# Attention and two mixture layers: scores of two tiles at once, steps in a new order, four first loads on ScalarE's queue

## The chip, the cores and the metric

The kernel runs on one core of a Trainium2 chip. A core has five engines with queues of their own: TensorE (PE: matmuls; PEld is its loading of weights), VectorE (DVE), ScalarE (ACT), GpSimd (POOL) and SyncE (SP, which here only issues DMAs). Each works through its instructions in order and waits for the others at semaphores; 16 DMA engines move data between memory (HBM) and the core's buffers. The metric is the time of one execution on the device in microseconds; lower is better.

## What is computed

Three layers follow each other. The first is attention within chunks of 64 positions, 8 batches of 8 heads; the second a soft mixture of experts over all 4608 tokens, whose two softmaxes run over tokens and over slots; the third a wide layer with a product of softmax and input and a normalization.

```python
scores = scale * np.matmul(q_c, k_c.transpose(0, 1, 2, 4, 3))
scores = scores - np.max(scores, axis=-1, keepdims=True)
attn = np.exp(scores)
attn = attn / (np.sum(attn, axis=-1, keepdims=True) + 1e-09)
out = np.matmul(attn, v_c)
...
logits = x @ phi
d = softmax of logits over tokens;  slot_input = d.T @ x
h = np.maximum(slot_input[e] @ w1[e], 0.0);  slot_out[e] = h @ w2[e]
x = softmax of logits over slots @ slot_out
...
h = x @ w_in;  solu = h * softmax(h)
ln = (solu - mean) / np.sqrt(var + 1e-06) * g_ln
out = ln @ w_out
```

## The kernel before

Tokens are cut into 36 tiles of 128 (`NT`), a tile holding two chunks for all 8 heads. A loop of 34 steps (L517) carries the attention in a software pipeline: in step i the scores of tile i are made, the probabilities of tile i-1 turned, the output x of tile i-2 made, and x of tile i-3 turned and multiplied with `phi`. Nothing reorders the work: each engine executes what the program text issues, in that order. Within a step the text's order is given by one of four lines of the table `STEP` (L29), taken in turn, so a pattern repeats every four steps. The names in a line are small functions, listed in `step_ops` (L471):

- `S` (TensorE) scores of a tile into the PSUM tile `s_ps`; `mx`, `sub` (VectorE) row maxima and their subtraction; `exp` (ScalarE); `PT` (TensorE) turns the probabilities and `PTe` (ScalarE) copies them out of PSUM; `x` (TensorE) multiplies with v; `rz` (ScalarE) copies the row sums, `rc` (VectorE) takes the reciprocal and `xm` (VectorE) multiplies; `xT`, `xTe` turn x and copy it.
- Every fourth step has work on a block of four tiles: `LT`, `lte`, `L`, `lall`, `tm`, `mT`, `mn`, `d`, `de`, `z`, `sl`, `acc`, which keep the running softmax over tokens and its weighted sum of x.
- `t`, `sq` (ScalarE), `u`, `a` (VectorE), `m`, `add`, `mul` (GpSimd) convert the third layer's weights, one chunk a step, from the tile `raw`.
- `qk`, `v`, `raw` and `W` issue loads on SyncE: q and k of tile i+4 (two DMAs of 256 KB), v of two tiles, two chunks of raw weights, and as many 512 KB loads of expert weights as the table `PACE` gives for the step.

The scores alternate between two banks of one PSUM tile `sx` (L249). `qk` may be issued when the scores that read the same one of four buffers are done. `FIRST` (L44) lists the loads ahead of the loop, all on SyncE. Behind the loop a list `ORDER` names the rest by hand: tiles 32 to 35, the experts (64 loads of weights, used by `h_ps` groups at L936, L973 and L987 up to 183 us), and from about 200 us the third layer, whose tiles are handled by a second loop at L1421.

Of the kernel before, what the change touches and what calls it, by code (L numbers as in the profile page):

```python
# [9 lines left out]
F32 = mybir.dt.float32  # L10
# [3 lines left out]
U32 = mybir.dt.uint32  # L14
# [3 lines left out]
PSUM = bass.MemoryType.PSUM  # L18
# [8 lines left out]


STEP = """  # L29
S a m t x xT u mT qk rz PT mx v xTe sub PTe W rc add mul raw exp xm mn d sq de  # L30
S a x u raw v m qk rz sl mx t W rc z xT sub xTe PT PTe add xm acc mul sq exp
m t S u a x qk rz xT mx W sub xTe PT rc acc v PTe add LT xm mul sq raw exp lte
t m a S x u raw L tm v mx xT add qk PT lall rz mul xTe sub rc PTe W sq xm exp
"""
PACE = [
    0, 0, 0, 0, 0, 0, 0, 1, 2, 2, 3, 4, 4, 5, 6, 6, 7, 8, 8, 9, 10, 10, 11, 12, 13, 13, 14, 15,
# [4 lines left out]
""".split()  # L41
AHEAD = 8
GATE = dict()
FIRST = "cs qk0 qk1 qk2 v0 raw0 qk3 g phi v2 raw2 raw4"  # L44
ORDER = """
cq1 cq2 cq3 cq4 cq5 cq6 cq7 S34 S35 loadw xT31 mx34 mx35 PT33 x32 xtev31 rz32 ptev33 sub34 LT31 lte7 ev32 own_c exp34
x33 own_q PT34 ptev34 xT32 L7 rz33 sub351 sub350 x34 exp350 PT350 exp351 ev33 xtev32 ptev0 xT33 PT351 lall7 LT32 rz34
# [20 lines left out]
def soft_moe_kernel(ctx: ExitStack, tc, qkT, v1, w12, w64, phi, g_ln, cst, out):  # L68
    nc = tc.nc
    ts = lambda i, n: slice(i * n, (i + 1) * n)  # L70

    def pool(name, bufs, stack=ctx, **kw):
        kw.setdefault("reuse_waits", "tile")
        return stack.enter_context(tc.tile_pool(name=name, bufs=bufs, **kw))
# [4 lines left out]
    cs = const.tile([128, 257], F32, name="cs")  # L79
# [5 lines left out]
    phi_sb = const.tile([128, 4, 32], F32, name="phi_sb")  # L85
    g_sb = const.tile([128, 8], F32, name="g_sb")
# [10 lines left out]
    lall = mp.tile([128, NT, 32], F32, name="lall")  # L97
    acc = mp.tile([128, 512], F32, name="acc")
# [6 lines left out]
    def mark(key, r):  # L105
        LAST[key] = r.ins.name

    def gated(what, r):
        key = GATE.get(what)
        if key in LAST:  # L110
            info = mybir.DependencyInfo(mybir.DependencyClass.Sync, mybir.DependencyReason.DATA)
            tc.add_manual_dep(r.ins, LAST[key], info, reason="even pace of loads")
# [45 lines left out]
    ps1 = pool("ps1", 1, p1, space=PSUM)  # L158
# [4 lines left out]
    qk = [cvp.tile([128, 3, 512], F32, name=f"qk{i}") for i in range(4)]  # L163
# [3 lines left out]
    vall = cvb.tile([128, 6, 520], F32, name="vall")  # L167
# [2 lines left out]
    zacc = kvp.tile([128, 1], F32, name="zacc")  # L170
    csum = kvp.tile([128, 512], F32, name="csum")

    def load_qk(t):
        if t < NT:
            for a in range(2):
                nc.sync.dma_start(out=qk[t % 4][a:128:2, a:a + 2, :], in_=qkT[t, a])


    def load_v(t):
        if t < NT and t % 2 == 0:  # L180
            gated("v", nc.sync.dma_start(out=vall[:, t % 6:t % 6 + 2, :].rearrange("p a d -> p (a d)"), in_=v1[t // 2]))

    raw_t = {}

    def load_raw(c):
        if c < NRAW and c % 2 == 0:
            raw = cvp.tile([128, 2, 256, 2], U32, tag="raw", name="raw", bufs=3)
            raw_t[c], raw_t[c + 1] = raw[:, 0], raw[:, 1]
            gated("raw", nc.sync.dma_start(out=raw.rearrange("p k n t -> p (k n t)"), in_=w64[c // 2].bitcast(U32)))

# [19 lines left out]
    def cv_u(c):  # L212
        mark("u", nc.vector.tensor_scalar(
            out=cv(c, "cu"), in0=cv_hi(c), scalar1=3, scalar2=0x3FFFFFF8, op0=ALU.logical_shift_left, op1=ALU.bitwise_and
        ))
# [11 lines left out]
    def cv_s(c):  # L227
        u = cvt["cu", c]
        nc.gpsimd.tensor_tensor(out=u, in0=u, in1=cvt["cr", c], op=ALU.add)  # L229
# [5 lines left out]
    def cv_c(c):  # L235
        nc.gpsimd.tensor_tensor(out=csum, in0=csum if c > 1 else wo[:, 0, :], in1=wo[:, c, :], op=ALU.add)

    first_loads = dict(
        qk0=lambda: load_qk(0), qk1=lambda: load_qk(1), qk2=lambda: load_qk(2), qk3=lambda: load_qk(3), v0=lambda: load_v(0), v2=lambda: load_v(2),
        **{f"raw{i}": lambda i=i: load_raw(i) for i in range(6)},  # L240
        cs=lambda: nc.sync.dma_start(out=cs, in_=cst), phi=lambda: nc.sync.dma_start(out=phi_sb, in_=phi),
        g=lambda: nc.sync.dma_start(out=g_sb, in_=g_ln),
    )
    for o in FIRST.split():
        first_loads[o]()

    p_t, pt_t, xps_t, x_t, lt_t, sps_t, mx_t = {}, {}, {}, {}, {}, {}, {}

    sx = ps1.tile([128, 2, 512], F32, name="s_ps")  # L249

    def pe_S(i):
        s = sx[:, i % 2, :]
        b = qk[i % 4]
        for g in range(4):
            for c in range(2):
                nc.tensor.matmul(  # L256
                    s[ts(c, 64), ts(g, 128)], b[:, 1, ts(2 * g + c, 64)], b[:, 0:3:2, ts(2 * g + c, 64)],
                    start=True, stop=True, tile_position=(0, 64 * c),
                )
        sps_t[i] = s.rearrange("p (h k) -> p h k", k=64)  # L260
# [28 lines left out]
    def x_view(x):  # L289
        return x[:, :, 0:260].rearrange("p a (g d) -> p a g d", d=65)  # L290

    def heads(x):
        return x.rearrange("p (g a d) -> p a g d", a=2, d=64)
# [8 lines left out]
    def x_sums(xp):  # L302
        rz = sm.tile([128, 2, 4, 1], F32, tag="rz", name="rz", bufs=4)
        nc.scalar.activation(out=rz, in_=xp[:, :, :, 64:65], func=AF.Copy, bias=1e-9)
        return rz
# [165 lines left out]
    def step_ops(i):  # L471
        s0, s1, s2, s3, s4 = (blk(n, i) for n in (6, 7, 8, 9, 10))
        if i == NT - 3:
            s4 = s3
        c = cstep.get(i, NRAW)
        st = {}

        def rz():
            st["xp"] = x_view(xps_t[i - 2])
            st["rz"] = x_sums(st["xp"])  # L480

        def rc():
            mark("rc", nc.vector.reciprocal(out=st["rz"], in_=st["rz"]))

        def xm():
            x_t[i - 2] = x = XB[(i - 2) % 7]
            mark("xm", nc.vector.tensor_tensor(
                out=heads(x), in0=st["xp"][:, :, :, 0:64],
                in1=st["rz"].to_broadcast([128, 2, 4, 64]), op=ALU.mult,
            ))  # L490

        def W():
            load_w(pace[i + 1] - pace[i])

        cvc, x2, x3 = c < NRAW, i >= 2, i >= 3
        return dict(
            u=(cvc, lambda: cv_u(c)), m=(cvc, lambda: cv_m(c)), a=(cvc, lambda: cv_a(c)), add=(cvc, lambda: cv_s(c)),
            mul=(cvc, lambda: cv_w(c)), raw=(cvc, lambda: load_raw(c + 5)),
            sq=(True, lambda: cv_sq(cstep.get(i + 1, NRAW))), t=(True, lambda: cv_t(cstep.get(i + 1, NRAW))),
            S=(True, lambda: pe_S(i)), qk=(True, lambda: load_qk(i + 4)),  # L500
            mx=(True, lambda: soft_max(i)), sub=(True, lambda: soft_sub(i)), exp=(True, lambda: exp_S(i)),
            PT=(i >= 1, lambda: PTm(i - 1)), PTe=(i >= 1, lambda: PTe(i - 1)),
            x=(x2, lambda: pe_x(i - 2)), v=(i >= 1, lambda: load_v(i + 3)),
            rz=(x2, rz), rc=(x2, rc), xm=(x2, xm),
            xT=(x3, lambda: xTm(i - 3)), xTe=(x3, lambda: xTe(i - 3)), LT=(x3, lambda: pe_LT(i - 3)),
            lte=(s0 is not None, lambda: blk_a(s0)),
            L=(s1 is not None, lambda: pe_L(s1)), lall=(s1 is not None, lambda: blk_l(s1)),
            tm=(s1 is not None, lambda: run_max(s1)),
            mT=(s2 is not None, lambda: mTm(s2)), mn=(s2 is not None, lambda: mnv(s2)),
            d=(s2 is not None, lambda: dv(s2)),  # L510
            de=(s2 is not None, lambda: de(s2)),
            z=(s3 is not None, lambda: zm(s3)), sl=(s3 is not None, lambda: slm(s3)),
            acc=(s4 is not None, lambda: blk_e2(s4)), W=(True, W),
        )
# [9 lines left out]
    n, last = NT - 1, NB - 1  # L524
# [53 lines left out]


    def x34():  # L580
        xps_t[n - 1] = x = sx
        pt = pt_t.pop(n - 1)
        for g in range(4):
            x_mm(n - 1, x, pt[:, g, :], g)
# [185 lines left out]
    def pt_pair():  # L770
# [79 lines left out]
    def sim(hf):  # L850
# [10 lines left out]
        out=siT,  # L861
# [415 lines left out]
    for n_ in range(2):  # L1277
# [18 lines left out]
        out=F["e1"], in_=F["h1"], func=AF.Exp, bias=F["nm1"][0], scale=1.0, accum_out=F["zz1"][:, 0:1]))  # L1296
# [201 lines left out]
```

## Time and profile before

| | us |
|---|---|
| median of 3 runs | 403.44 (402.84 to 403.8) |
| the profiled execution | 402.77 |
| its span, first to last instruction | 401.0 |

The page says of the span: TensorE is busy for 382.4 us, VectorE 311.0, ScalarE 224.3, GpSimd 200.2; 70.60 MB are read from HBM. In the slices a digit is the busy share in tenths of one fortieth of the span, 10 us. Matmul records overlap in a pipeline, so that the start of one group to the start of the next is the better measure of what a group costs TensorE than its own duration; a group of scores has 16 records.

### The profile page before, as it was taken

The page shows a single profiled execution, that of the slowest core. Times are in us where ns is not written, and L with a number is a line of the kernel's source. Part 1 is how long each engine was busy: PE and PEld are TensorE (multiplying, and loading weights), DVE is VectorE, ACT ScalarE, POOL GpSimd, SP SyncE. Part 2 cuts the span into 40 slices and gives each one's busy share as a digit, 9 for nine tenths or more (in the row PEclk, how much of TensorE's full clock was granted, in tenths as well). Part 3 has the DMA queues.
Part 4 walks back from the last instruction along what each step waited for, and adds up shares of the span by engine and source line. Part 5 has one row for each costly group of instructions (what it writes and reads, how often), then busy time and mean ns, then how long its engine had stood idle before and what let it go on. Part 6 is the DMA issues. An engine that isn't in the chain of part 4 may idle for free. (4 is left out here: it accounts for less than half of the span.)

```text
span 401.0 us, 10317 instructions
## 1 busy us (share of the span) xinstructions
PE 382.4 (95%) x3947; PEld 220.4 (55%) x3947; DVE 311.0 (78%) x777; ACT 224.3 (56%) x470; POOL 200.2 (50%) x201
## 2 busy tenths in 40 slices
PE   3799899999999999999999999999999999999997
PEld 2577777777787642354544444444444444444445
DVE  3788788989886449574989799999888888888840
ACT  1577877877785512332577765556554555455521
POOL 2577767777778246330123255555455544454430
PEclk9999999999999999999999999999999999999999
DMA  7999999999999999991156757777665666557671
GB/s 231 403 409 408 389 397 397 409 407 407 410 397 408 401 396 406 409 391 26 30 103 146 140 134 159 159 158 148 144 140 135 144 151 133 132 137 158 132 159 52
DMA packets 101153, 99.20 MB, mean 247 GB/s; under 512 B 78064, under 2 KB 78704, under 8 KB 101104
## 3 DMA queue, kind: packets, MB, share of 16 engines
q1 hardware_dynamic: 101104, 98.54, 77.1%
q8 instruction: 31, 0.51, 0.5%
q14 instruction: 18, 0.15, 0.1%
HBM read 70.60 MB, written 9.44 MB: 200 GB/s over the span
## 5 line engine op out<-in xcount | busy, mean ns | idle before, releaser
L1194 POOL TENSOR_SCALAR uh<-u,sc 128x1024 f16<-128x1024 f32 (+1 forms) x35 | 65.1, 1860 | 51.1 <-issue 38.3
L1393 PEld LDWEIGHTS <-uhT 128*128 128x128 f16 x560 | 52.1, 98 | 68.3 <-issue 8.8
L1393 PE MATMUL o_ps<-xb,uhT 128*128 128x512 f16 x280 | 66.7, 380 | 0.7 <-DMA uhT<-uh 0.7
L1393 PE MATMUL o_ps<-xb,ulT 128*128 128x512 f16 x280 | 66.3, 379 | 0.0
L1393 PE MATMUL o_ps<-wo,uhT 128*128 128x512 f16 x280 | 66.1, 379 | 0.0
L1322 ACT ACTIVATE e<-h_ps,nm 128x1024 f32<-128x1024 f32 x34 | 37.8, 1113 | 43.7 <-DVE nm L1316 43.7
L1210 ACT ACTIVATE e<-u,nmean 128x1024 f32<-128x1024 f32 x35 | 40.1, 1147 | 28.7 <-DVE nmean L1209 28.7
L256 PE MATMUL s_ps<-qk 128*64 128x128 f32 x576 | 41.1, 287 | 9.3 <-DMA qk<-in_qkT 6.5
L1360 POOL TENSOR_TENSOR a<-a,mhalf 128x1 f32<-128x1 f32 x36 | 21.8, 606 | 56.2 <-DVE a L1377 42.5
L1316 DVE TENSOR_REDUCE nm<-h_ps 128x1 f32<-128x1024 f32 x34 | 41.5, 1220 | 9.3 <-PE h_ps L1311 9.3
L1185 DVE SCALAR_TENSOR_TENSOR u<-h_ps,e 128x1024 f32<-128x1024 f32 x35 | 42.8, 1223 | 6.1 <-ACT e L1322 6.1
L1393 PEld LDWEIGHTS <-ulT 128*128 128x128 f16 x280 | 27.3, 98 | 33.1 <-issue 0.3
L1370 DVE SCALAR_TENSOR_TENSOR ul<-u,sc,uh 128x1024 f16<-128x1024 f32 x35 | 45.3, 1295 | 0.0
L256 PEld LDWEIGHTS s_ps<-qk 128*64 128x64 f32 x576 | 32.5, 141 | 16.2 <-issue 10.3
L398 ACT ACTIVATE xt_b<-xt_ps 128x512 f32<-128x512 f32 (+1 forms) x37 | 21.6, 586 | 17.8 <-PE xt_ps L416 16.9
L265 DVE TENSOR_REDUCE mx<-s_ps 128x8 f32<-128x512 f32 x36 | 24.6, 684 | 8.5 <-PE s_ps L256 8.0
L1411 ACT ACTIVATE ob<-o_ps,a 128x512 f32<-128x512 f32 x35 | 23.8, 679 | 9.3 <-PE o_ps L1393 8.0
L219 POOL TENSOR_SCALAR conv<-conv 128x256 f32<-128x256 f32 x16 | 17.6, 1099 | 21.8 <-ACT conv L206 21.8
L1311 PE MATMUL h_ps<-s,c4T 128*128 128x512 f32 x68 | 27.4, 485 | 0.0
L277 ACT ACTIVATE p<-p 128x512 f32<-128x512 f32 x35 | 21.7, 621 | 6.6 <-DVE p L271 6.6
L271 DVE TENSOR_TENSOR p<-s_ps,mx 128x512 f32<-128x512 f32 x35 | 24.1, 690 | 0.9
L229 POOL TENSOR_TENSOR conv<-conv 128x256 int32<-128x256 int32 x32 | 23.3, 729 | 2.6
(232 smaller groups left out, 633.5 us busy)
## 6 DMA issues: line engine op xcount, KB each, us to landing
w<-in_w SPq DMA_DIRECT2D x45, 512.0 KB, 8.0
qk<-in_qkT SPq DMA_DIRECT2D x72, 256.0 KB, 6.8
vall<-in_v SPq DMA_DIRECT2D x18, 520.0 KB, 6.7
out<-ob SPq DMA_DIRECT2D x35, 256.0 KB, 2.1
raw<-in_w SPq DMA_DIRECT2D x16, 512.0 KB, 6.4
qk<-in_w SPq DMA_DIRECT2D x4, 512.0 KB, 9.0
w_raw<-in_w SPq DMA_DIRECT2D x3, 512.0 KB, 9.0
vall<-in_w SPq DMA_DIRECT2D x3, 512.0 KB, 8.9
```

Of the source, the lines that this page charges most:

```text
L256: nc.tensor.matmul(s[ts(c, 64), ts(g, 128)], b[:, 1, ts(2 * g + c, 64)], b[:, 0:3:2, ts(2 * g + c, 64)], start=True, stop=True, tile_posit ...
L265: mark("mx", nc.vector.tensor_reduce(out=mx, in_=s, axis=AX.X, op=ALU.max))
L271: mark("sub", nc.vector.tensor_tensor(out=p, in0=s, in1=mx.unsqueeze(2).to_broadcast([128, 8, 64]), op=ALU.subtract,))
L1185: nc.vector.scalar_tensor_tensor(out=u, in0=d["h"], scalar=1.0, in1=e, op0=ALU.mult, op1=ALU.mult, accum_out=zz[:, 1:2])
L1194: nc.gpsimd.tensor_scalar(out=uh[:, 0:n], in0=u[:, 0:n], scalar1=d["sc"][:, 1:2], scalar2=1.0, op0=ALU.mult, op1=ALU.mult)
L1210: nc.scalar.activation(out=d["e"], in_=d["u"], func=AF.Square, bias=nmean, scale=1.0, accum_out=d["zz"][:, 2:3])
L1311: nc.tensor.matmul(h[:, ts(n, 512)], c4T[:, i, :], s4[n], start=True, stop=True)
L1316: nc.vector.tensor_reduce(out=nm, in_=st[i]["h"], axis=AX.X, op=ALU.max, negate=True)
L1322: nc.scalar.activation(out=d["e"], in_=d["h"], func=AF.Exp, bias=d["nm"], scale=1.0, accum_out=d["zz"][:, 0:1])
L1370: nc.vector.scalar_tensor_tensor(out=ul, in0=d["u"], scalar=d["sc"][:, 1:2], in1=d["uh"], op0=ALU.mult, op1=ALU.subtract)
L1393: nc.tensor.matmul(d["o"], lt(n % 8), w(n % 8), start=(n == 0), stop=(n == 23))
L1411: nc.scalar.activation(out=ob, in_=d["o"], func=AF.Copy, scale=d["a"][:, 7:8])
```

## The change

`S` is now called in even steps only and makes the scores of tiles i and i+1, one behind the other; each has a PSUM tile of its own (`s0` and `s1`, in a pool `ps_s`). The pool is closed ahead of the x of tile 34 and one with the old tile `sx` opened in its place. All four lines of `STEP` have a new order. Of the first loads, q and k of tiles 2 and 3 go into ScalarE's queue (marked `*`), and three loads leave the list: the second v and raw are issued right behind the q and k of step 0, the third raw behind those of step 1 (`THEN`).

```diff
 STEP = """
-S a m t x xT u mT qk rz PT mx v xTe sub PTe W rc add mul raw exp xm mn d sq de
-S a x u raw v m qk rz sl mx t W rc z xT sub xTe PT PTe add xm acc mul sq exp
-m t S u a x qk rz xT mx W sub xTe PT rc acc v PTe add LT xm mul sq raw exp lte
-t m a S x u raw L tm v mx xT add qk PT lall rz mul xTe sub rc PTe W sq xm exp
+S x t v m a rz xT u qk xTe PT mT PTe mx W sub add rc exp mul xm mn sq d raw de
+S mx xT qk x PT a u sub z m W raw add PTe rz sl exp t rc mul xm v acc xTe sq
+S m mx t x u W a acc xT rz PT xTe raw add LT mul sub rc PTe v sq exp lte qk xm
+x u S qk a m v t add rz mx sub xT L raw PT tm PTe rc xTe mul xm lall sq exp W
 """
...
-FIRST = "cs qk0 qk1 qk2 v0 raw0 qk3 g phi v2 raw2 raw4"
+FIRST = "cs qk0 qk1 qk2* v0 raw0 qk3* g phi"
+THEN = {0: 'v2 raw2', 1: 'raw4'}
...
-                nc.sync.dma_start(out=qk[t % 4][a:128:2, a:a + 2, :], in_=qkT[t, a])
+                queue[0].dma_start(out=qk[t % 4][a:128:2, a:a + 2, :], in_=qkT[t, a])
...
     for o in FIRST.split():
-        first_loads[o]()
+        queue[0] = nc.scalar if o[-1] == "*" else nc.sync
+        first_loads[o.rstrip("*")]()
+    queue[0] = nc.sync
...
-    sx = ps1.tile([128, 2, 512], F32, name="s_ps")
+    pss = ctx.enter_context(ExitStack())
+    ps_s = pool("ps_s", 1, pss, space=PSUM)
+    s_banks = [ps_s.tile([128, 512], F32, name="s_ps", tag=f"s{a}") for a in range(2)]
+    sx = None
...
-        s = sx[:, i % 2, :]
+        s = s_banks[i % 2]
...
+        def q():
+            load_qk(i + 4)
+            for o in THEN.get(i, "").split():
+                first_loads[o]()
...
-            S=(True, lambda: pe_S(i)), qk=(True, lambda: load_qk(i + 4)),
+            S=(i % 2 == 0, lambda: (pe_S(i), pe_S(i + 1))), qk=(True, q),
...
     def x34():
+        nonlocal sx
+        pss.close()
+        sx = pool("ps_sx", 1, pss, space=PSUM).tile([128, 2, 512], F32, name="s_ps")
```

In the rows of order that follow, a name with a number is one buffer (`qk0_111` is the buffer of every fourth tile's q and k), and xN is how many instructions of the kind stand in a row; the line numbers of the changed kernel are some 8 higher.

TensorE in the loop, the first two steps of a pattern of four, before: one group of scores at the front of each step.

```order
L256 MATMUL s_ps_148<-qk0_111 64x128 x8
L282 MATMUL x_ps_1121<-vall_123,pt_1103 64x65 x16
L416 MATMUL xt_ps_1138<-cs_60,xb6_86 128x128 x4
L423 MATMUL mT_ps_1144<-cs_60,ltb_149 128x128
L407 MATMUL pt_ps_1150<-cs_60,p_1100 128x128 x4
L256 MATMUL s_ps_148<-qk1_112 64x128 x8
L282 MATMUL x_ps_1188<-vall_123,pt_1160 64x65 x16
L467 MATMUL sl_ps_1214<-xb1_81,d_1170 32x512
```

The same two steps on TensorE after:

```order
L264 MATMUL s_ps_146<-qk0_111 64x128 x8
L264 MATMUL s_ps_147<-qk1_112 64x128 x8
L290 MATMUL x_ps_1130<-vall_123,pt_1103 64x65 x16
L424 MATMUL xt_ps_1152<-cs_60,xb6_86 128x128 x4
L415 MATMUL pt_ps_1161<-cs_60,p_1086 128x128 x4
L431 MATMUL mT_ps_1166<-cs_60,ltb_148 128x128
L424 MATMUL xt_ps_1193<-cs_60,xb0_80 128x128 x4
L290 MATMUL x_ps_1200<-vall_123,pt_1168 64x65 x16
L415 MATMUL pt_ps_1217<-cs_60,p_1174 128x128 x4
L469 MATMUL lt_ps_1028<-cs_60,d_1183 128x1
L475 MATMUL sl_ps_1235<-xb1_81,d_1183 32x512
```

The second scores have moved to the front of the first step, and the second step begins with the turning of `xb0_80`, made from the x of the step before, which used to stand behind x, sl and z.

SyncE at the start, before, from the constants to the q and k of tile 4 (which go to the buffer `qk0_111` again):

```order
L241 DMA cs_60<-in_cst 128x257
L176 DMA qk0_111<-in_qkT 64x1024 x2
L176 DMA qk1_112<-in_qkT 64x1024 x2
L176 DMA qk2_113<-in_qkT 64x1024 x2
L181 DMA vall_123<-in_v1 128x1040
L189 DMA raw_137<-in_w64 128x1024
L176 DMA qk3_114<-in_qkT 64x1024 x2
L242 DMA g_sb_62<-in_g_ln 128x8
L241 DMA phi_sb_61<-in_phi 128x128
L181 DMA vall_123<-in_v1 128x1040
L189 DMA raw_144<-in_w64 128x1024
L189 DMA raw_146<-in_w64 128x1024
```

SyncE at the start after, up to the q and k of tile 5 (buffer `qk1_112`) and the third raw:

```order
L244 DMA cs_60<-in_cst 128x257
L179 DMA qk0_111<-in_qkT 64x1024 x2
L179 DMA qk1_112<-in_qkT 64x1024 x2
L184 DMA vall_123<-in_v1 128x1040
L192 DMA raw_137<-in_w64 128x1024
L245 DMA g_sb_62<-in_g_ln 128x8
L244 DMA phi_sb_61<-in_phi 128x128
L179 DMA qk0_111<-in_qkT 64x1024 x2
L184 DMA vall_123<-in_v1 128x1040
L192 DMA raw_173<-in_w64 128x1024
L179 DMA qk1_112<-in_qkT 64x1024 x2
L192 DMA raw_184<-in_w64 128x1024
```

Tiles 2 and 3 are gone from the queue, and tile 4 has moved ahead of the second v and raw; before, it stood behind the last row shown.

ScalarE at the start, after:

```order
L179 DMA qk2_113<-in_qkT 64x1024 x2
L179 DMA qk3_114<-in_qkT 64x1024 x2
L285 ACT_TABLE_LOAD
L285 ACTIVATE p_177<-p_177 128x512
L406 ACTIVATE pt_193<-pt_ps_186 128x512
L285 ACTIVATE p_191<-p_191 128x512
```

The four DMAs of tiles 2 and 3 stand ahead of everything else there; before, the table load was first.

## Rows read from the trace of the kernel before

**Rows 1.** Page, part 2: busy tenths of 40 equal slices.

```profile
PE   3799899999999999999999999999999999999997
...
DVE  3788788989886449574989799999888888888840
...
DMA  7999999999999999991156757777665666557671
```

**Rows 2.** Chain of waits in order of time: start us, us, what.

```profile
206.86 5.35 PE o_ps L1393 x24
```

**Rows 3.** Tile w, loads issued from 171.5 us: ns min/median/max, first and last start.

```profile
L128 SPq DMA_DIRECT2D w<-in_w x1: 328/328/328, 171.9 to 171.9; - x1
...
DMA to landing us min/median/max: 10.4/10.4/10.4
```

**Rows 4.** Timeline of PE, 180 to 184 us: start us, us, engine, line, operation.

```profile
182.63 1.08 PE L987 MATMUL h_ps<-w,hTb 128*4 128x128 f32 x32
183.50 1.06 PE L1112 MATMUL sw_ps<-wi,soT 128*32 128x512 f32 x8
```

**Rows 5.** Windows: stretch, us, busy of PE, PEld, DVE, ACT, POOL, clock, DMA share, GB/s.

```profile
2.50:5.00 2.50, 0.00 (x0) 0.00 (x0) 0.48 (x1) 0.00 (x0) 0.20 (x3) 1.00 0.81 270
5.00:7.50 2.50, 1.97 (x16) 1.60 (x16) 0.33 (x1) 0.00 (x0) 0.00 (x0) 1.00 1.00 282
15.00:20.00 5.00, 3.54 (x69) 2.85 (x70) 3.74 (x8) 2.96 (x7) 4.12 (x5) 1.00 1.03 414
40.00:50.00 10.00, 8.95 (x201) 7.55 (x198) 7.94 (x18) 8.01 (x22) 7.26 (x10) 1.00 1.00 389
```

**Rows 6.** Timeline of SP's queue, 0 to 24 us.

```profile
1.44 3.75 SPq L176 DMA_DIRECT2D qk<-in_qkT  x6
...
12.59 1.12 SPq L176 DMA_DIRECT2D qk<-in_qkT  x2
```

**Rows 7.** Timeline of all engines, 4 to 24 us: scores of tiles 0, 4, 5.

```profile
5.16 1.97 PE L256 MATMUL s_ps<-qk 128*64 128x128 f32 x16 [5.16 <-DMA qk<-in_qkT]
...
7.17 0.69 DVE L265 TENSOR_REDUCE mx<-s_ps 128x8 f32<-128x512 f32 x1 [4.13 <-PE s_ps L256]
...
19.39 1.09 PE L256 MATMUL s_ps<-qk 128*64 128x128 f32 x16 [1.01 <-DMA qk<-in_qkT]
...
22.46 1.09 PE L256 MATMUL s_ps<-qk 128*64 128x128 f32 x16 [0.33 <-DMA qk<-in_qkT]
```

**Rows 8.** Timeline of PE, 101 to 126 us: steps late in the loop.

```profile
102.54 1.09 PE L256 MATMUL s_ps<-qk 128*64 128x128 f32 x16
103.57 0.70 PE L282 MATMUL x_ps<-vall,pt 64*64 64x65 f32 x32
104.20 0.66 PE L416 MATMUL xt_ps<-cs,xb 128*128 128x128 f32 x4
...
104.80 0.60 PE L407 MATMUL pt_ps<-cs,p 128*128 128x128 f32 x4
105.33 1.09 PE L256 MATMUL s_ps<-qk 128*64 128x128 f32 x16
...
116.37 1.09 PE L256 MATMUL s_ps<-qk 128*64 128x128 f32 x16
...
123.37 1.97 PE L256 MATMUL s_ps<-qk 128*64 128x128 f32 x32
125.27 0.66 PE L416 MATMUL xt_ps<-cs,xb 128*128 128x128 f32 x4
```

**Rows 9.** Page, part 6: loads, count, size, median us from issue to landing.

```profile
qk<-in_qkT SPq DMA_DIRECT2D x72, 256.0 KB, 6.8
```

**Rows 10.** Groups by line, 20 to 120 us: busy, mean ns | idle before.

```profile
L487 DVE TENSOR_TENSOR xb<-x_ps,rz 128x512 f32<-128x512 f32 x29 | 19.9, 687 | 1.8
...
L483 DVE RECIPROCAL rz<-rz 128x8 f32<-128x8 f32 x29 | 5.6, 192 | 0.0
...
L304 ACT ACTIVATE rz<-x_ps 128x8 f32<-128x8 f32 x29 | 4.9, 170 | 0.6 <-PE x_ps L282 0.4
```

More of the change, by code (lines that the diff above doesn't have):

```diff
@@ L171, in soft_moe_kernel @@
     csum = kvp.tile([128, 512], F32, name="csum")
+    queue = [nc.sync]
     def load_qk(t):
@@ L175, in load_qk @@
             for a in range(2):
-                nc.sync.dma_start(out=qk[t % 4][a:128:2, a:a + 2, :], in_=qkT[t, a])
+                queue[0].dma_start(out=qk[t % 4][a:128:2, a:a + 2, :], in_=qkT[t, a])
     def load_v(t):
         if t < NT and t % 2 == 0:
-            gated("v", nc.sync.dma_start(out=vall[:, t % 6:t % 6 + 2, :].rearrange("p a d -> p (a d)"), in_=v1[t // 2]))
+            gated("v", queue[0].dma_start(out=vall[:, t % 6:t % 6 + 2, :].rearrange("p a d -> p (a d)"), in_=v1[t // 2]))
     raw_t = {}
@@ L188, in load_raw @@
             raw_t[c], raw_t[c + 1] = raw[:, 0], raw[:, 1]
-            gated("raw", nc.sync.dma_start(out=raw.rearrange("p k n t -> p (k n t)"), in_=w64[c // 2].bitcast(U32)))
+            gated("raw", queue[0].dma_start(out=raw.rearrange("p k n t -> p (k n t)"), in_=w64[c // 2].bitcast(U32)))
     cvt = {}
@@ L239, in soft_moe_kernel @@
         qk0=lambda: load_qk(0), qk1=lambda: load_qk(1), qk2=lambda: load_qk(2), qk3=lambda: load_qk(3), v0=lambda: load_v(0), v2=lambda: load_v(2),
-        **{f"raw{i}": lambda i=i: load_raw(i) for i in range(6)},
-        cs=lambda: nc.sync.dma_start(out=cs, in_=cst), phi=lambda: nc.sync.dma_start(out=phi_sb, in_=phi),
-        g=lambda: nc.sync.dma_start(out=g_sb, in_=g_ln),
+        **{f"raw{i}": lambda i=i: load_raw(i) for i in range(6)}, v4=lambda: load_v(4), v6=lambda: load_v(6),
+        cs=lambda: queue[0].dma_start(out=cs, in_=cst), phi=lambda: queue[0].dma_start(out=phi_sb, in_=phi),
+        g=lambda: queue[0].dma_start(out=g_sb, in_=g_ln),
     )
     for o in FIRST.split():
-        first_loads[o]()
+        queue[0] = nc.scalar if o[-1] == "*" else nc.sync
+        first_loads[o.rstrip("*")]()
+    queue[0] = nc.sync
     p_t, pt_t, xps_t, x_t, lt_t, sps_t, mx_t = {}, {}, {}, {}, {}, {}, {}
-    sx = ps1.tile([128, 2, 512], F32, name="s_ps")
+    pss = ctx.enter_context(ExitStack())
+    ps_s = pool("ps_s", 1, pss, space=PSUM)
+    s_banks = [ps_s.tile([128, 512], F32, name="s_ps", tag=f"s{a}") for a in range(2)]
+    sx = None
     def pe_S(i):
-        s = sx[:, i % 2, :]
+        s = s_banks[i % 2]
         b = qk[i % 4]
@@ L872, in open_2 @@
         nonlocal e1, ps2, soT, cz, mx
+        pss.close()
         p1.close()
```

## The prediction

> **What bounds the kernel now.** I read the slices of the page first [rows 1]: from the second slice (10 us) to 180 us both the PE row and the DMA row stand at 9 nearly throughout; after that DMA falls to 1 while PE stays at 9. So two resources are full together in the first 180 us, and TensorE alone afterwards. The chain of waits shows the second part: from 206.86 us [rows 2] to the end it is TensorE work without a gap, so whatever moves the point at 183 us moves the end one for one, and every step that the change touches lies before it. The question is which of the two full resources sets that point.
>
> The answer is in the last expert weights. The view of the tile `w` [rows 3] shows the last load issued at 171.9 us and landed 10.4 us later, at 182.3 us. The timeline of TensorE [rows 4] shows the last group on these weights at 182.63 us, 32 matmul records for two loads, and the next group at 183.50 us: the half on the last load starts at 182.63 + 0.87 / 2 = 183.07 us. TensorE comes 0.8 us after the data. Both reach the point almost together, TensorE the later by 0.8 us: a faster loop on TensorE is worth 0.8 us and no more, unless the load stream ends earlier too; a slower loop costs its whole length.
>
> **Where the load stream loses time.** Once it runs it moves 414 GB/s. At the start it is slower [rows 5]: 270 and 282 GB/s in the stretches of 2.5 us from 2.5 and from 5 us. Against 414 that is 2.5 x (144 + 132) / 414 = 1.7 us lost. In the stretch from 40 us it moves 389, a loss of 10 x 25 / 414 = 0.6 us. The bytes are the same before and after, so the stream's end can come forward by what it regains here, 0 to 2.3 us.
>
> **The change, part by part.**
>
> Q and k of tiles 2 and 3 on ScalarE. SyncE issues the first six q/k loads one after another in 3.75 us, 0.63 us each [rows 6]. Four of the first eight now leave ScalarE's queue at the same time. There they take 4 x 0.63 = 2.5 us in front of the table load; the first exp waits for scores that begin at 5.16 us and for VectorE, which begins on them at 7.17 [rows 7], so ScalarE's cost is hidden; without that cover it would be the 2.5 us. On SyncE the two loads of tile 2 stood ahead of the first v and raw, those of tile 3 behind them; all four leave. What two queues do to the slow start no row shows. Bounds: the whole 1.7 us gained, or 0.6 us lost (one load of tile 2, 0.63 us, ahead of tile 1's). I take 0.5 us gained, nearer to nothing: from 5 to 7.5 us the rate is 282 GB/s although all six loads have been issued, so more loads in flight have not helped there.
>
> What that row shows is a slow start with enough issued. The Trainium skill, page "DMA: Bandwidth & Descriptors", section "Issuing engines are not separate DMA queues", says that loads started from several engines run on the same 16 DMA engines and that only issuing time is saved. By that rule the 0.5 us is zero; it stands behind the second rival.
>
> New order of the first loads. Before, the loads of tile 4 were issued at 12.59 us [rows 6], behind the second v and two raws; its scores started at 19.39 us and those of tile 5 at 22.46 us, both with the data as releaser [rows 7]. After, tile 4 goes ahead of that v and both raws, and tile 5 ahead of one raw and one v that preceded it: for tile 5 512 + 520 KB, 2.6 us at 414 GB/s, so its scores can start at about 19.9 us. As both scores stand at the front of the step now, the x, xT and PT that lay between them are still to do then: 103.57 to 105.33 us in a later step, 1.76 us with a small mT [rows 8], 1.7 us without. TensorE is ahead by 2.6 - 1.7 = 0.9 us. Later pairs should find their data: the second tile of a pair is used three steps after its load's issue and not four. Four steps are 116.37 - 102.54 = 13.83 us, three 10.4, and a q/k load lands in 6.8 us [rows 8, 9].
>
> Pairs of scores. A lone group of scores takes TensorE 1.03 us to the start of the x behind it (102.54 to 103.57); the pair of tiles 34 and 35, the only one before, takes 1.90 us (123.37 to 125.27) [rows 8]. That is 2.06 - 1.90 = 0.16 us for each of 17 pairs, 2.7 us; or half, 1.4 us, if only the first of the two saves. I take 2.1 us. Each score has a bank and a tile of its own now, and the second waits for the subtraction of the tile before, which lies about a step back on VectorE: nothing.
>
> The new order of the steps. In the second step of four xT now stands first, on the x of the step before. Between that x and it, TensorE has xT, PT and mT of older tiles, 1.76 us [rows 8]. Meanwhile the data goes through the x group itself, 0.70, rz on ScalarE, 0.17, the reciprocal, 0.19, and the multiplication, 0.69, on VectorE [rows 8, 10]: 1.75 us, and four hand-overs. One hand-over, from the end of the first scores (5.16 + 1.97) to VectorE at 7.17, is 0.04 us [rows 7]; with four it is 1.91 us, and a wait of 0.15 us falls on TensorE once in four steps. Queued behind it are the next x, PT, z and sl, for which ScalarE's PTe and VectorE's acc wait. Eight times makes 1.2 us: nothing if VectorE is early, more if it is late (rival 1). Raw loads, which wait for VectorE, move behind q/k and W in the second and fourth steps, so that q/k no longer stand behind that wait in SyncE's queue. That may give back part of the 0.6 us at 40 us; I take 0.2 us (0 to 0.6). The new pool for the x of tile 34 is taken after the subtractions of tile 35, which that operation waited for already: nothing.
>
> **Sum.** TensorE is ahead at the last weights by 0.9 + 2.1 - 1.2 = 1.8 us (3.6 with no wait and the full saving; behind, in rival 1). The load stream allows 0.8 + 0.5 + 0.2 = 1.5 us (0.2 to 3.1). The smaller counts, 1.5 us. The profiled execution took 402.77 us, so it would take 401.3; the median of the three runs, 403.44, stands 0.7 us above it, and from there the same step gives **401.9 us**. About 0.2% (0.8 us) is what a measurement of this kernel can tell from no change: below 402.6 is faster, above 404.2 slower.
>
> **Rivals.**
> 1. The waits of the new order eat the saving (slower). For: the moved xT has no slack by the sum above, and VectorE, which delivers to it, stands at 7 to 9 tenths in the loop [rows 1]. Against: in the steady steps before, TensorE's groups follow each other without idle time [rows 8]. It decides from a wait of (0.9 + 2.1) / 8 = 0.37 us per four steps; at 0.6 us TensorE is 4.8 - 3.0 = 1.8 us late, which counts in full: 405.2 us. Chance 0.18.
> 2. The second queue saves only issuing time, and the stream ends at 182.3 us as it did. TensorE then waits for the last weights and only the 0.8 us is gained: 402.6 us, on the bound between faster and same. For: 282 GB/s with six loads issued [rows 5]. Against: other tensors now come between the q/k. Chance 0.20, half to either side.
> 3. The change doesn't do what it says: the pairs come apart, because the second tile's data is late when SyncE can't issue at once, and saving and waits cancel: 403.4 us. For: three steps are less than four; against: 10.4 us against 6.8. Chance 0.12.
> 4. The slow start closes wholly: 0.8 + 1.7 + 0.6 = 3.1 us, within TensorE's 3.6: 400.3 us. Chance 0.10.
>
> **How the numbers follow.** My forecast has the remaining 0.40, with a range of its own from 401.0 to 402.8, of which 0.04 lies in "same". Faster: 0.36 + 0.10 + 0.10 = 0.56. Same: 0.04 + 0.10 + 0.12 = 0.26. Slower: 0.18. The range goes from 400.6, within rival 4, to 404.8, within rival 1; about half of each is left out, 0.14.
>
> **What would show it.** Right: the last load of `w` lands near 181.6 us and TensorE's half on it starts with no lead left; the scores of tile 5 start near 20 us; pairs take 1.9 us; the part from 206 us is the same but for its place. Wrong on the side of the stream: the start still moves 270 to 290 GB/s and the last landing stays at 182.3. Wrong on the side of TensorE: xT waits for VectorE by more than 0.37 us in every second step of four, with the last weights landed over 1 us before use. A change of time that arises after 206 us would overthrow the whole argument.

## The result: 0.6% slower, and where it went

The changed kernel takes 405.81 us (405.01 to 406.96, 8 runs) against 403.62 us in the runs beside it; the ratio is 1.0058, interval 1.0042 to 1.0075. That is slower, and 1.0 us above the range that was forecast. The profiled execution took 406.3 us, its span is 404.5 us, 3.5 us more than that of the kernel before. The slices of the page (10 us each) look much as in [rows 1]:

```profile
PE   2999989899999999999989999999999999999997
...
DMA  7999999999999999990176666677766666567671
```

TensorE and the DMA engines are still full together up to 180 us. The point to compare is the last expert weights. The view of the tile `w` from 171.5 us (operation, count, duration in ns, first and last start) and the timeline of TensorE (start us, us) show it:

```profile
L129 SPq DMA_DIRECT2D w<-in_w x2: 328/328/328, 172.0 to 173.2; - x2
...
DMA to landing us min/median/max: 10.1/10.1/10.1
```

```profile
185.29 1.08 PE L1004 MATMUL h_ps<-w,hTb 128*4 128x128 f32 x32
186.16 1.06 PE L1129 MATMUL sw_ps<-wi,soT 128*32 128x512 f32 x8
```

The last load lands at 173.2 + 10.1 = 183.3 us, 1.0 us later than in [rows 3]; TensorE's half on it starts at 185.29 + 0.87 / 2 = 185.73 us, 2.7 us later than in [rows 4]. The data wait for TensorE for 2.4 us where it was 0.8. So 2.7 of the 3.5 us are lost by TensorE before this point, and not by the stream of loads. The other 0.8 us come later, most of them between 200 and 210 us, where the first `uhT` (a turn by DMA) takes longer to land: TensorE waits 1.5 us for it, while the kernel before waits 0.7 us at the second one and the changed kernel does not. The first turn before, the same after, and TensorE's wait after:

```profile
L1203 SPq DMA_TRANSPOSE uhT<-uh x1: 1232/1232/1232, 197.3 to 197.3; - x1
...
DMA to landing us min/median/max: 3.1/3.1/3.1
```

```profile
L1220 SPq DMA_TRANSPOSE uhT<-uh x1: 1232/1232/1232, 199.9 to 199.9; - x1
...
DMA to landing us min/median/max: 4.6/4.6/4.6
```

```profile
204.56 1.90 PE L1410 MATMUL o_ps<-xb,uhT 128*128 128x512 f16 x8 [1.48 <-DMA uhT<-uh]
```

### The profile page after: what moved, and what is told of

The parts are those of the page before. It is cut to its first block, busy times and chain, and to the rows that moved or that the text cites. A ratio compares the mean times of both kernels' runs of the same rounds, so it can differ in the third digit from the quotient of the medians.

```text
span 404.5 us, 10333 instructions
## 1 busy us (share of the span) xinstructions
PE 383.2 (95%) x3947; PEld 222.7 (55%) x3947; DVE 313.1 (77%) x777; ACT 223.9 (55%) x470; POOL 200.1 (49%) x201
## 4 chain that ended last, share of the span: by engine, by line
PE 72%; DMA 9%; issue 7%; DVE 5%; POOL 3%; ACT 2%; SPq 0%; DVEq 0%; ACTq 0%; POOLq 0%
PE o_ps L1410 44%; DMA qk<-in_qkT 8%; PE s_ps L264 5%; PE h_ps L1328 4%; PE h_ps L953 3%; PE x_ps L290 3%; PE xt_ps L424 3%; PE pt_ps L415 2%; PE h_ps L990 2%; POOL xb L1096 1%; DVE xb L500 1%; PE lt_ps L333 1%; PE o_ps L1420 1%; DMA uhT<-uh 1%; DVE p L279 1%
## 5 line engine op out<-in xcount | busy, mean ns | idle before, releaser
L1211 POOL TENSOR_SCALAR uh<-u,sc 128x1024 f16<-128x1024 f32 (+1 forms) x35 | 64.0, 1830 | 51.1 <-issue 38.3
L264 PE MATMUL s_ps<-qk 128*64 128x128 f32 x576 | 38.9, 290 | 8.6 <-DMA qk<-in_qkT 7.6
L264 PEld LDWEIGHTS s_ps<-qk 128*64 128x64 f32 x576 | 33.8, 146 | 16.9 <-issue 10.6
L406 ACT ACTIVATE pt<-pt_ps 128x512 f32<-128x512 f32 x35 | 20.9, 597 | 14.2 <-PE pt_ps L415 14.2
L290 PE MATMUL x_ps<-vall,pt 64*64 64x65 f32 x1088 | 24.6, 225 | 2.6 <-issue 1.7
L424 PE MATMUL xt_ps<-cs,xb 128*128 128x128 f32 x140 | 22.8, 284 | 3.5 <-DVE xb L500 2.6
```

The source lines that it names most:

```text
L264: nc.tensor.matmul(s[ts(c, 64), ts(g, 128)], b[:, 1, ts(2 * g + c, 64)], b[:, 0:3:2, ts(2 * g + c, 64)], start=True, stop=True, tile_posit ...
L290: nc.tensor.matmul(x[ts(c, 64), a, ts(g, 65)], pt[ts(a, 64), ts(c, 64)], vall[ts(a, 64), i % 6, ts(2 * g + c, 65)], start=True, stop=True, ...
L406: A=lambda o, i: nc.scalar.activation(out=o, in_=i, func=AF.Copy),
L424: nc.tensor.transpose(t[:, g, :], x_t[i][:, ts(g, 128)], ident)
L1211: nc.gpsimd.tensor_scalar(out=uh[:, 0:n], in0=u[:, 0:n], scalar1=d["sc"][:, 1:2], scalar2=1.0, op0=ALU.mult, op1=ALU.mult)
```

## Experiments

Two places of the changed kernel's trace gave the theories. The first is the wait that the forecast had named. In the timeline from 107 us, the chain from an x group to the xT made of it:

```profile
107.03 0.70 PE L290 MATMUL x_ps<-vall,pt 64*64 64x65 f32 x32
...
107.79 0.18 ACT L312 ACTIVATE rz<-x_ps 128x8 f32<-128x8 f32 x1
108.00 0.20 DVE L496 RECIPROCAL rz<-rz 128x8 f32<-128x8 f32 x1 [0.31 <-ACT rz L312]
...
108.31 0.69 DVE L500 TENSOR_TENSOR xb<-x_ps,rz 128x512 f32<-128x512 f32 x1
...
109.14 0.63 PE L424 MATMUL xt_ps<-cs,xb 128*128 128x128 f32 x4 [0.29 <-DVE xb L500]
```

From the start of x to xT it is 2.11 us, and TensorE has 1.66 us of other work meanwhile (mT starts at 108.58 and takes 0.11 to the next start): a wait of 0.45 us. **Theory A** says that this wait loses the time. The second place is a stall in the middle of an x group, where nothing is waited for:

```profile
102.44 0.58 PE L290 MATMUL x_ps<-vall,pt 64*64 64x65 f32 x24
103.72 0.35 PE L290 MATMUL x_ps<-vall,pt 64*64 64x65 f32 x8 [0.70 <-issue]
```

Of the DMA packets of 101.2 to 102.5 us one is of another kind (queue, kind: packets, MB, share of 16 engines):

```profile
q1 hardware_dynamic: 138, 0.51, 98.3%
q8 instruction: 1, 0.02, 5.3%
```

It is read here as a block of TensorE's own program. The page counts 31 of them, 0.51 MB in all, for 3947 matmuls and as many weight loads: that is some 64 bytes an instruction and 16 KB, or some 126 matmul records, to a block. This one's packet lies at 101.33 to 102.44 us, and TensorE goes on 1.28 us after its end. The stalls of over 0.3 us inside a group of matmuls stand at matmul records 341, 467, 718, 843, 1221, 1724 and 2226, at multiples of 125.6 from each other: at the borders between blocks. (At 1221, between the two scores of a pair, the profile names an instruction of VectorE as releaser that the scores do not use. A shorter one, 0.3 us at 1473 between two groups, it puts down to a q/k load, though the last of these had landed 4 us earlier.) **Theory B** says that TensorE loses its time there, because blocks arrive late through DMA engines that are full of data. **Theory C** puts it on the new first loads.

The table gives for each run the median in us, the interval of its ratio to the kernel before, and two numbers of the profiled execution. "Loop" is the time in us from the start of tile 8's scores to the start of tile 34's. The last column has TensorE's stalls in the loop at borders, how many and how long together: the excess over the usual distance between two such matmuls, counted at a border where it is over 0.25 us and ends 1.15 to 1.75 us after a block's packet. So loops and stalls are of one execution each. In parentheses stand single executions whose total is of no interest.

| kernel | median | ratio | loop | stalls at borders |
|---|---|---|---|---|
| before | 403.6 | | 90.6 | 1, 0.6 us |
| changed | 405.8 | 1.0042 to 1.0075 | 93.4 | 6, 4.4 us |
| before_flat | (425.4) | | 90.2 | 0 |
| after_flat | (422.9) | | 90.1 | 0 |
| old_single_flat | (426.3) | | 91.0 | 3, 1.4 us |
| old_single | 406.0 | 1.0028 to 1.0072 | 93.9 | 4, 3.5 us |
| old_tiles | 406.0 | 1.0043 to 1.0083 | 93.4 | 4, 2.9 us |
| old_star | 405.8 | 1.0016 to 1.0057 | 92.0 | 4, 2.0 us |
| old_sync | 406.2 | 1.0014 to 1.0072 | 93.3 | 4, 2.8 us |
| start_only | 404.5 | 0.9989 to 1.0025 | 91.0 | 1, 1.0 us |
| after_oldstart | 406.4 | 1.0037 to 1.0172 | 92.7 | 5, 3.4 us |
| old_pair | 410.5 | 1.0125 to 1.0235 | 98.5 | 2, 2.1 us |
| new_single | 415.4 | 1.0255 to 1.0343 | 99.1 | 6, 4.7 us |
| pt_first | 407.5 | 1.0083 to 1.0121 | 92.8 | 6, 3.8 us |
| after_onetile | 414.9 | 1.0230 to 1.0287 | 97.1 | 3, 1.8 us |
| after_shift | 407.1 | 1.0051 to 1.0114 | 91.9 | 3, 2.0 us |
| before_shift | 404.0 | 0.9988 to 1.0023 | 91.0 | 2, 1.2 us |

### Slack for the DMA engines

Both kernels were run with no expert weights loaded in the loop:

```diff
-PACE = [
-    0, 0, 0, 0, 0, 0, 0, 1, 2, 2, 3, 4, 4, 5, 6, 6, 7, 8, 8, 9, 10, 10, 11, 12, 13, 13, 14, 15,
-    16, 16, 17, 18, 19, 22, 25, 25,
-]
+PACE = [0] * 34 + [25, 25]
```

> The kernel before with no expert weights loaded during the loop (PACE is 0 up to step 33), so that the DMA engines have slack there; all loads still happen, some 16 us later, and the total is of no interest. Its partner is the changed kernel with the same edit; what counts is the start of the scores of tile 34, 123.4 us in the kernel before. Theory B (TensorE's program itself arrives late through the full DMA engines): the program blocks land early, the few stalls of 0.3 to 0.6 us behind a block vanish, scores of tile 34 at about 122 us. Theory A (the moved xT waits for VectorE): no change to speak of, 123 to 123.5 us.

> The changed kernel with no expert weights loaded during the loop; in the changed kernel the scores of tile 34 start at 126.0 us, 2.7 us behind the kernel before. Theory B: the six stalls of 0.47 to 1.11 us that follow a program block's landing (4.9 us together) vanish, scores of tile 34 at about 121.2 us, at or ahead of its partner. Theory A: xT waits 0.44 us in every fourth step as before, and tile 34 stays 2 to 2.7 us behind the partner, with the long stalls still there. Theory C (the new first loads cost): the lag is there by 30 us and stays.

The windows of the changed kernel with this edit, 25 to 120 us, show the slack: 315 GB/s where the changed kernel moves 400 (last columns: clock, DMA share, GB/s):

```profile
25.00:120.00 95.00, 91.34 (x1830) 73.09 (x1829) 83.34 (x207) 72.48 (x193) 73.63 (x84) 1.00 0.90 315
```

The scores of tile 34 start at 123.18 and at 122.98 us; without the edit it was 123.37 and 126.03. The lag of 2.7 us is gone with the data that filled the DMA engines, and with it all six stalls of the loop. The blocks come earlier too: a packet starts on average 1.9 us (before_flat) and 2.0 us (after_flat) after TensorE crosses the border ahead of its block, and 3.4 and 4.1 us with the engines full. What TensorE still waits for in 24 to 124 us, of the two in this order (what waited, for what: us in total, times, longest):

```profile
PE sl_ps L464 <- ACT d L445: 1.0, 4, 0.3
PE s_ps L253 <- DVE p L268: 0.6, 2, 0.3
PE lt_ps L322 <- ACT zacc L377: 0.3, 1, 0.3
```

```profile
PE xt_ps L421 <- DVE xb L497: 3.4, 7, 0.6
PE L_ps L361 <- ACT ltb L346: 0.3, 1, 0.3
```

So A is there too: xT's wait takes as much as pairs and order save, the loops are equal at 90.2 and 90.1 us, and none of the 2 us that was expected remains. What makes the changed kernel slower than the one before comes with full DMA engines: 93.4 - 90.1 = 3.3 us, where the kernel before pays 90.6 - 90.2 = 0.4. Theory B holds for this part, with one execution of each kernel with slack.

### The first loads, and a part that was thought free

The new first loads were put into the kernel before, with its order and single scores. This version also had the changed kernel's separate PSUM tiles for the scores.

```diff
-FIRST = "cs qk0 qk1 qk2 v0 raw0 qk3 g phi v2 raw2 raw4"
+FIRST = "cs qk0 qk1 qk2* v0 raw0 qk3* g phi"
+THEN = {0: 'v2 raw2', 1: 'raw4'}
...
-    sx = ps1.tile([128, 2, 512], F32, name="s_ps")
+    s_banks = [ps_s.tile([128, 512], F32, name="s_ps", tag=f"s{a}") for a in range(2)]
```

> The kernel before with the new first loads alone (tiles 2 and 3 on ScalarE's queue, second v and raw behind tile 4): order of the steps and single scores as before, only each score with a PSUM tile of its own. Theory C: 405 us or more, most of the 2.2 us. Theories A and B: within 0.5 us of the kernel before (403.1 to 404.1).

405.96 us: as theory C has it. But its loop is as long as the changed kernel's, 93.9 us, with four stalls at borders, while the scores of tile 6 start at 24.98 us, no later than before (25.27). Four runs took it apart; the first has the slack of above, the second the tiles alone, the third the tiles and ScalarE's queue, the fourth the tiles and the later loads on SyncE:

```diff
-FIRST = "cs qk0 qk1 qk2* v0 raw0 qk3* g phi"
-THEN = {0: 'v2 raw2', 1: 'raw4'}
+FIRST = "cs qk0 qk1 qk2 v0 raw0 qk3 g phi v2 raw2 raw4"
+THEN = {}
```

(that of old_tiles; old_star keeps the two `*` in it, old_sync is the first pair of lines without them)

> The kernel before with the new first loads, and no expert weights loaded during the loop; partner of the two runs with the same edit. Scores of tile 34 started at 123.2 us in the kernel before with that edit, and at 126.9 us in the kernel with the new first loads and its normal weight loads. Theory B (stalls behind program blocks): within 0.5 us of 123.2. Theory C (the first loads delay the data themselves): 125 us or more.

> The kernel before with nothing changed but a PSUM tile for each of the two scores. If these tiles carry the 2.4 us: 405 us or more. Theories B and C: 403.0 to 404.0 us, as the kernel before.

> The kernel before with q and k of tiles 2 and 3 in ScalarE's queue, and the second v and the raws where they were. If the second queue carries the cost: 405 to 406 us. If the loads put behind tiles 4 and 5 carry it: 403.0 to 404.0 us.

> The kernel before with the second v and raw behind tile 4's q and k and the third raw behind tile 5's, and all first loads on SyncE. If these places carry the cost: 405 to 406 us; if the second queue does: 403.0 to 404.0 us.

The tiles alone cost 2.5 us (old_tiles), the rest adds nothing that can be told from it. With slack the lag of this version (old_single), 3.5 us at tile 34, falls to 123.72 - 123.18 = 0.5 us, though three stalls of 1.4 us together remain at borders: slack takes most of the loss, not all. The timeline of TensorE in the kernel with the tiles alone shows the same stall, inside an x group and without a releaser:

```profile
102.86 0.57 PE L290 MATMUL x_ps<-vall,pt 64*64 64x65 f32 x20
104.18 0.45 PE L290 MATMUL x_ps<-vall,pt 64*64 64x65 f32 x12 [0.76 <-issue]
```

Then the first loads with the one tile of before, and the changed kernel with one tile:

```diff
-        s = s_banks[i % 2]
+        s = sx[:, i % 2, :]
```

> The kernel before with the new first loads alone, the scores in their one PSUM tile with two banks as before. If the separate tiles carried the cost of the runs above: 403.0 to 404.0 us. If the first loads cost something of their own, as theory C says: 404.5 us or more.

> The changed kernel with both scores of a pair in the two banks of one PSUM tile, so that a pair waits for VectorE's subtraction of the tile before. If the separate tiles carry the loss here too: 403 to 404.5 us. If pairs and order lose it by themselves (long stalls behind blocks as in the changed kernel): 405.3 to 406.5 us.

With one tile the first loads cost nothing that can be told from noise: ratio 1.0007. Theory C falls. For the pairs one tile is no way out: 414.9 us. Now VectorE's maxima of the first tile wait for the end of both scores (the pair of 104.15 us ends at 106.1):

```profile
106.16 0.69 DVE L270 TENSOR_REDUCE mx<-s_ps 128x8 f32<-128x512 f32 x1 [1.24 <-PE s_ps L261]
```

and TensorE then for VectorE; its waits from 25 to 125 us:

```profile
PE xt_ps L421 <- DVE xb L497: 5.0, 7, 0.9
PE x_ps L287 <- DVE xb L497: 3.0, 4, 0.8
```

The changed kernel with the old first loads says the same from the other side:

> The changed kernel with the first loads of the kernel before (all on SyncE, second v and third raw ahead of the loop): pairs and new order alone. Theory C: the new first loads alone cost 2.4 us, so without them 403.4 us or less. Theory B: no fixed price of the first loads; they set how the loads of the loop lie against TensorE's blocks, and long stalls appear here too: 404.5 to 407 us. Theory A: 405.8 us as the changed kernel.

406.4 us, no better than with the new ones (405.8 to 406.8 us in three runs, 411.0 in the fourth).

### Order and pairs

> New first loads and scores in pairs, but the order of the other operations as in the kernel before. Theory A: the saving of the pairs without the wait of the moved xT: 401.5 to 402.5 us. Theory B: TensorE runs faster against the same arrival of its program and meets long stalls behind blocks, 403.5 to 406 us. Theory C: as the run with the new first loads alone.

> The changed kernel with the scores made one tile a step (each at the place of S in the new order), new first loads kept. Theory A: the moved xT waits as in the changed kernel and the saving of the pairs, 0.13 us each or 2.2 us, is gone: 407.5 to 409 us. Theory B: TensorE runs slower against its program blocks and meets fewer long stalls; part of the 2.2 us comes back: 405 to 407.5 us.

Pairs in the old order (410.5 us) and single scores in the new order (415.4 us) are both far worse than either kernel, so pairs and order belong together. In the first x waits for the copy of PT, which the score between them used to cover:

```profile
PE x_ps L290 <- ACT pt L406: 5.3, 7, 0.8
```

Then the changed kernel with the wait of xT taken away:

```diff
-S x t v m a rz xT u qk xTe PT mT PTe mx W sub add rc exp mul xm mn sq d raw de
-S mx xT qk x PT a u sub z m W raw add PTe rz sl exp t rc mul xm v acc xTe sq
+S x t v m a rz PT u qk PTe xT mT xTe mx W sub add rc exp mul xm mn sq d raw de
+S mx qk x xT PT a u sub z m W raw add PTe rz sl exp t rc mul xm v acc xTe sq
```

> The changed kernel with PT ahead of xT in the first step of four and x ahead of xT in the second, so that xT has the time of a PT, an mT and an x group more. Theory A: its wait of 0.44 us in every four steps falls to 0.1 to 0.2 us, eight times, 2 to 2.5 us: 403.3 to 403.9 us. Theory B: the waits go, but TensorE then reaches its block borders earlier and waits there: 404.5 to 406 us.

407.5 us. xT waits no more, but x now waits for PT's copy (PT 0.60 and PTe 0.60 us against xT and mT beside them), and the stalls at borders are as before:

```profile
PE x_ps L290 <- ACT pt L406: 1.3, 5, 0.3
PE x_ps L290 <- issue: 1.3, 3, 0.7
PE x_ps L290 <- DVE xb L500: 1.0, 2, 0.6
PE xt_ps L424 <- issue: 0.9, 1, 0.9
PE pt_ps L415 <- issue: 0.8, 2, 0.5
```

### Moving the borders

```diff
+    for _ in range(24):
+        nc.tensor.matmul(s_banks[1][0:32, 0:1], ident[:, 0:32], ones, start=True, stop=True)
```

(in the kernel before the output is `sx[0:32, 1, 0:1]`)

> The changed kernel with 24 tiny matmuls (32x1, from the constants) ahead of the first scores on TensorE: 48 more matmul records, which shift every later border between TensorE's program blocks by 48 matmuls in the program; the tiles wait for nothing new. Theory B: the long stalls again end 1.2 to 1.7 us after a block's packet, and still at matmul records 341 + 125.6 m counted with the 48, so at other operations of the program than in the changed kernel; their sum changes (2 to 6 us) and the total with it, 404.5 to 407.5 us. Theory A: the stalls stay with the moved xT, and the total stays at 405.8 within 0.5 us.

> The kernel before with 24 tiny matmuls (48 records) ahead of its first scores, so that all later borders of TensorE's program blocks lie 48 matmuls earlier in the program. Theory B in its strong form (the kernel before meets few stalls only because its borders lie well against its loads): long stalls appear at records 341 + 125.6 m and the time rises to 404.5 to 407 us. In its weak form (the blocks land 2.1 us ahead of their border on average there and 1.5 us in the changed kernel, and the margin decides): the time stays at 403.4 within 0.5 us.

In the changed kernel the two longest stalls came at records 971 and 1851 with the 48 counted, 341 + 5 x 126 and 341 + 12 x 125.8: they stay at the borders and leave the operations. Their sum fell to 2.0 us in the profiled execution, which was the quickest of its runs (404.81 us; median 407.06). The kernel before stays what it was (ratio 1.0006): it does not owe its time to a lucky place of its borders, and the strong form of B falls.

### Fewer bytes in flight

A dependency of each load in the loop on an earlier load kept the bytes in flight under a limit.

```diff
+            left = LIM - kb
+            for name, k in reversed(flight):
+                left -= k
+                if left < 0:
+                    tc.add_manual_dep(r.ins, name, info, reason="bytes in flight")
+                    break
```

> The changed kernel, where in the loop a load is issued only when it and the loads not yet landed are at most 2048 KB (in the changed kernel some 2800 KB are in flight, 8 loads at most). Theory B: a program block waits in proportion to the bytes ahead of it, 4.2 us fall to about 3.2; the stalls behind blocks fall from 4.9 us to under 1.5, the scores of tile 34 start at 122.5 to 124 us (126.0 in the changed kernel) and the total is 402.5 to 404.5 us if the loads still move 400 GB/s. Theory A: no change of the stalls, 405.8 us or more.

> The same with at most 1536 KB in flight. Theory B: blocks wait about 2.4 us, no long stall, scores of tile 34 at 122 to 123.5 us; whether three loads in flight keep the DMA engines full is open: if they move 390 GB/s instead of 400, the last weights land 4 us later and the total is 406 us or more. Theory A: 405.8 us or more with the stalls unchanged.

> The kernel before with at most 2048 KB in flight in the loop. Theory B: its few stalls of 0.3 to 0.6 us go too, 0.5 us in all in front of the scores of tile 34 (123.4 us); the last weights set the end, so 402.6 to 403.6 us. Theory A: 403.4 us, the same.

These do not test theory B: they took 429.9, 453.5 and 428.6 us. From 25 to 120 us the first moves 334 GB/s where the changed kernel moves 400, and scores wait for their data:

```profile
25.00:120.00 95.00, 81.93 (x1573) 64.93 (x1565) 70.72 (x174) 60.90 (x163) 61.88 (x71) 0.96 0.95 334
```

```profile
PE s_ps L278 <- DMA qk<-in_qkT: 9.1, 10, 2.8
```

The kernel before has 2.8 MB in flight in the mean, and with 2 MB the engines here run dry. Stalls of 2.0 and 2.1 us at borders came all the same, so bytes in flight are not all that delays a block.

### What is settled and what is open

Two things are shown. Most of the loss needs full DMA engines and lies at the borders of TensorE's blocks. And of the parts of the change it is the separate PSUM tiles that bring it into the kernel before (old_tiles, and old_single against start_only), while the first loads bring nothing. In the changed kernel the tiles can't be taken out for a test of their own, because one tile costs it 9 us, as TensorE then waits for VectorE (after_onetile).

Taking the stalls out of the loops by subtraction, the changed kernel's would be 89.0 us against 90.0: by this sum pairs and order save TensorE 1.0 us, and stalls of 4.4 us take its place (0.6 before).

How little room a block has can be estimated. Its packet starts 3.4 us after TensorE has crossed the border ahead of it in the kernel before and 4.1 us in the changed one (means of 14), takes 1.1 us, and after a late one TensorE goes on 1.2 us after its end at the earliest: 5.7 and 6.4 us together. A mean block is 125.6 / 268 x 13.83 = 6.5 us of work (268 records are a pattern of four steps), and the two quickest, from 82.9 and 95.7 us of the kernel before, are 5.4 us. These two end at records 1471 and 1723, where nearly all the kernels with two tiles stall. By this estimate hardly any room is left for a faster loop. It takes the crossing of the border for the moment at which the next block is asked for; that is not shown, and with slack one packet starts 1.0 us ahead of the crossing.

Open is why blocks come in time when scores wait for VectorE's last subtraction (one tile, in the kernel before and its variants: 1 or 2 stalls of 0.6 to 1.2 us in three kernels) and late when they do not (two tiles: 4 stalls of 2.0 to 3.5 us in each of four kernels with the same order), since this wait is only 0.6 to 0.7 us in all. In the mean the tiles alone delay a block little (from 3.4 to 3.5 us); it is single blocks that come late. That the wait is the cause and not, say, the place of the tiles in PSUM was not separated.

## Why the prediction was wrong, point by point

- **What bounds the kernel.** Right as far as it went: both limits meet at 183 us, and what TensorE loses there counts in full. (In the second slice the PE row has 7 and not the 9 that was read, which changes nothing.) The third supply, TensorE's program, was not looked at, though the page of before has its row of packets.
- **The start of the stream.** 0.5 us were taken, 0 came. The windows of after (columns as in [rows 5]):

```profile
2.50:5.00 2.50, 0.00 (x0) 0.00 (x0) 0.48 (x1) 0.00 (x0) 0.20 (x3) 1.00 0.80 231
5.00:7.50 2.50, 1.97 (x16) 1.60 (x16) 0.34 (x1) 1.28 (x1) 0.00 (x0) 1.00 0.91 346
7.50:10.00 2.50, 0.60 (x6) 0.63 (x8) 1.04 (x2) 0.63 (x1) 0.00 (x0) 1.00 1.00 401
10.00:12.50 2.50, 2.50 (x20) 1.84 (x18) 1.06 (x2) 0.04 (x1) 0.00 (x0) 1.00 0.99 344
```

  From 5 to 10 us it moves more (346 and 401 GB/s, before 282 [rows 5] and 323), ahead and behind less; over 20 us it is the same within 0.1 MB. Rival 2 had this right, and so had the Trainium skill, page "DMA: Bandwidth & Descriptors", section "Issuing engines are not separate DMA queues": a second issuing engine saves issuing time alone. The trace agrees: 6.30 MB in the first 20 us, before 6.35. ScalarE's cost was hidden, as said.
- **The stream later.** 0.2 us were to come back, and at 40 to 50 us more did: 406 GB/s for 389, 0.4 us. But the last landing is 1.0 us later, for more is lost in another place:

```profile
60.00:70.00 10.00, 9.71 (x188) 7.82 (x188) 8.66 (x22) 8.08 (x23) 7.64 (x9) 1.00 0.97 343
```

  SyncE issues nothing for 3 us there: a v load (L184) waits 2.8 us, from 57.8 us, for the x group that starts at 60.12 us; TensorE reaches it late, as the x group ahead of it had stalled for 1.0 us at a border at 56.4. This is the queue behind a waiting load that the forecast named for raw loads and not for v.
- **Tile 5's scores** start at 20.20 us, forecast 19.9: right. The 0.9 us did not last: the first moved xT waits for VectorE, tile 6 starts at 25.21 us against 25.27, and after a stall of 0.6 us at a border (record 341, 29.87 us) tile 8 starts at 32.66 against 32.74.

```profile
23.44 0.63 PE L424 MATMUL xt_ps<-cs,xb 128*128 128x128 f32 x4 [0.55 <-DVE xb L500]
```

- **Pairs.** 0.16 us each, the full saving, and the pairs hold together (rival 3 did not come about); late in the loop it is 113.93 - 112.03 = 1.90 us from the pair to x:

```profile
112.03 1.97 PE L264 MATMUL s_ps<-qk 128*64 128x128 f32 x32
113.93 0.46 PE L290 MATMUL x_ps<-vall,pt 64*64 64x65 f32 x16
```

- **The moved xT.** Mis-sized: 0.15 us forecast, 0.45 measured, beyond the 0.37 from which rival 1 decides. The hand-overs take 0.06, 0.03, 0.11 and 0.14 us and not 0.04 each, and TensorE's cover is 1.66 and not 1.76 us; with slack, when the loop keeps its pace, VectorE is in a subtraction as the row sums come, and the wait grows to 0.72 us in the step at 92.1 us (0.83 from mT to xT, less 0.11) and to 0.65 us in the mean of seven.
- **"Each score has a bank and a tile of its own now: nothing."** This is the step that failed most. Run alone in the kernel before the tiles cost 2.5 us, by a way (stalls at block borders) that no rival held. In the changed kernel the sum has no term for such stalls, and they take 4.4 us of the loop where they took 0.6. Rival 1 came near in time, 405.2 us, with half of the mechanism.
- **The sum for TensorE.** It was to be 1.8 us ahead at the last weights and is 2.7 us behind, a difference of 4.5 us. The stalls make 3.8 of it and the longer wait of xT 8 x 0.30 = 2.4; the full saving of the pairs gives back 0.6, and two waits of the kernel before that are gone (of `sl` for `d`, 0.9, and of scores for the subtraction, 0.6) give 1.5. That is 4.1 us, an estimate of its make-up and not a measurement of each part.
- **After 206 us** nothing was to change; the loss at the first `uhT` goes with a program block too: its packet (202.07 to 202.95 us) lies beside the turn. In the twenty traces of this case the turn takes 4.5 to 4.8 us to land in the nine that have a packet beside it, and 3.1 us in the eleven that have none.

## What to carry to other kernels

Where TensorE runs many short matmuls beside full DMA engines, its program can be a third supply: compare the time of a block's worth of instructions with what a block takes to arrive before paying for a faster loop. A wait that is removed is an edit with a price to be bounded on both sides, even where it is hardly seen in the trace; run it alone. And run parts one at a time down to the smallest: the first loads looked guilty until the tile that came with them was taken out.

## What the runs showed of the hardware

TensorE's instructions come in blocks of 16 KB, by DMA packets from 19 to 390 us of the execution (31 in the changed kernel). The packets are later when data fill the DMA engines: they start 3.4 to 4.1 us after TensorE crosses the border ahead, against 1.9 to 2.0 us with slack. Stalls behind late ones were 0.3 to 1.1 us in the changed kernel, and 2.1 us at most in the kernels run here (after_lim2048). In the profile such a stall mostly stands as "issue" in the middle of a group of matmuls that had all they needed. The first `uhT` lands 1.4 to 1.7 us later where such a packet lies beside it (4.5 to 4.8 us for 3.1).
